# Head pairs taken two at a time: scores, exponentials and softmax sums by quads in a fused attention and MLP kernel

**Chip, cores, metric.** One core of a Trainium2 chip. The metric is device microseconds (us) of one execution; lower is better. Every timing below is a median of several executions, beside executions of the kernel before on the same chip; an execution more than 1.5% above the fastest of its kernel is called slow and left out of the ratios.

## The reference

Soft-capped attention over 8 batches of 12 heads (448 tokens, head dimension 64), then an MLP over all 3584 tokens (width 768, inner width 1024).

```python
scores = scale * np.matmul(q, k.transpose(0, 1, 3, 2))
scores = cap * np.tanh(scores / cap)
attn = np.exp(scores - max)            # then divided by its sum
attn_out = np.matmul(attn, v)
x = attn_out.transpose(0, 2, 1, 3).reshape(B * S, H * D)
h1, h2 = x @ w1, x @ w2
out = np.maximum(h1, h2) @ w_out
```

The kernel uses max(h1, h2) = relu(x(w1 - w2)) + x w2, and multiplies w2 by w_out beforehand. So the MLP has a gate-up product with w1 - w2 (`wd_sb`), a relu, and two output products (`wm_sb`, `wo_sb`).

## The kernel before

A *pair* is two heads, one on each half of the 128 partitions; there are 48. In the traces every engine works through its own instructions in program order. The program interleaves attention with a queue of filling matmuls: `F(n)` emits the next n matmuls of the MLP (early on: of the preparation of the weights). Of the 448 keys of a head, three chunks of 128 are used whole; the last 64 keys of both heads share one chunk.

```python
def qk(i, j):                         # scores of chunk j of pair i, then tanh
    ...
    if j < NJ:
        for h in range(2):            # two row halves at once
            nc.tensor.matmul(s[:, h, :S], t[r, j*P:(j+1)*P], qTn[r, :])
        nc.scalar.activation(tanh[i][:, TJ[j]:TJ[j]+2, :], s[:, :, :S], AF.Tanh, ...)
    else:                             # shared last chunk
        nc.tensor.matmul(s[:, 0, :S], t[:, 3*P:4*P], qTn)
        nc.scalar.activation(tanh[i][:, TJ[j], :], s[:, 0, :S], AF.Tanh, ...)

def add(i, step):                     # sums of exponentials on VectorE, from pair 9 on
    if step == 0:   nc.vector.tensor_add(esum[i], e[:, 0:2, :], e[:, 2:4, :])
    elif step < 3:  nc.vector.tensor_add(esum[i][r, h, :], esum[i][r, h, :], e[r, TJ[3], :])  # 64 rows
    else:           nc.vector.tensor_add(esum[i], esum[i], e[:, TJ[2]:TJ[2]+2, :])
# pv(i): PV product into ps[:, 0], sums (all-ones matmul) into ps[:, 1]
# pv_out(i): VectorE copies both into U[group of three pairs]

def gather(g):                        # once per three pairs
    nc.sync.dma_start(out=sums, in_=<one row of U per head>)
def invert(g):                        # reciprocal, then to DRAM
    nc.vector.reciprocal(rec_s, sums);  nc.sync.dma_start(out=rec_d, in_=rec_s)
def spread(g):                        # read back, broadcast over 64 partitions
    eng = nc.gpsimd if g < 2 else nc.sync
    eng.dma_start(out=rec_b[...], in_=<rec_d>.to_broadcast(...))
def normalize(g):                     # GpSimd: xT = U * rec_b
    ...
for i in range(N):                    # main loop, cut
    qk(i+1, 2); ex(i+1, 5, 7); pv(i); pv_out(i)
    if n == G-1: gather(g)            # n = i % 3
    F(5); add(i+1, 0); <loads, casts, transposing loads of later pairs>
    F(4); add(i+1, 1); F(3); add(i+1, 2); qk(i+2, 0); qk(i+2, 1)
    F(6); add(i+1, 3)
    if n == 0: invert(g-1); spread(g-1)
    if n == 1: normalize(g-1)
    qk(i+2, 3); ex(i+2, 0, 5); F(7)
```

## Time and profile before

| | before |
|---|---|
| median of 4 runs beside the changed kernel | 389.3 us (387.9 to 391.5) |
| profiled execution, first to last instruction | 390.3 us (392.1 device us, 2.8 above the median) |
| VectorE (DVE) busy | 265.8 us, 68% |
| start of the short exponential of the twelfth pair | 87.3 us |
| 34 later pairs, from 101.9 to 333.2 us | 231.3 us |

The two last rows come from the start times of the exponentials on ScalarE (ACT). The first marks the end of the early part, in which inputs and weights still arrive. The prediction shows the main lines of this profile. Columns of all views of waits: us in total, number, longest.

### The profile page before, as it was taken

What the parts mean: (1) busy time and instruction counts of PE and PEld (TensorE: products, weight loads), DVE (VectorE), ACT (ScalarE), POOL (GpSimd) and SP (SyncE); (2) the same over time, 40 slices, a digit from 0 to 9 for tenths busy, and PEclk for the clock granted to TensorE, in tenths of its full rate; (3) what the DMA queues carried; (4) which work ended last, traced back from release to release, by engine and by line L of the source; (5) the groups of instructions that cost most, each with busy time, mean ns of one, the idle gap of its engine ahead of it and who ended that gap; (6) DMA issues with size and microseconds to landing.
All of it is one profiled execution on the core that took longest, in us unless ns stands there. A gap on an engine that the chain in (4) does not pass through costs nothing.

```text
span 390.3 us, 6492 instructions
## 1 busy us (share of the span) xinstructions
PE 354.5 (91%) x2449; PEld 170.0 (44%) x2449; DVE 265.8 (68%) x401; ACT 290.2 (74%) x289; POOL 157.6 (40%) x191
## 2 busy tenths in 40 slices
PE   2667999799998999999988999999979999989995
PEld 1223555443443444444433444444434444455563
DVE  4431687998779676987788588886877867833521
ACT  3899899697998799888986999889987999200000
POOL 3464165773436442725454363534453421320000
PEclk9997999999999999999999999999999999999999
DMA  7999899465979567977797488969794851422021
GB/s 230 266 254 219 289 288 249 124 164 145 235 208 256 154 157 220 230 233 193 199 238 206 101 238 237 251 151 239 207 200 129 161 146 45 113 72 114 9 82 81
DMA packets 100391, 71.55 MB, mean 183 GB/s; under 512 B 58248, under 2 KB 93192, under 8 KB 100360
## 3 DMA queue, kind: packets, MB, share of 16 engines
q1 hardware_dynamic: 98088, 66.62, 65.0%
q0 software_dynamic: 2272, 4.52, 5.8%
q8 instruction: 19, 0.31, 0.4%
q14 instruction: 12, 0.10, 0.1%
HBM read 53.48 MB, written 11.18 MB: 166 GB/s over the span
## 4 chain that ended last, share of the span: by engine, by line
PE 56%; DVE 23%; ACT 10%; DMA 7%; SPq 1%; issue 1%; POOL 1%; DVEq 0%; POOLq 0%; ACTq 0%
PE mm L418 12%; PE mm L403 11%; PE mm L415 10%; PE pv L328 6%; PE s L288 6%; DVE u L347 5%; DVE esum L311 5%; ACT expo L295 5%; ACT tanh L289 4%; DVE esum L307 4%; PE pv L336 3%; DVE gT L407 3%; PE pv L335 3%; DMA rec_b<-rec_d 2%; PE mm L235 2%; DVE esum L313 2%
## 5 line engine op out<-in xcount | busy, mean ns | idle before, releaser
L289 ACT ACTIVATE tanh<-s 128x896 bf16<-128x896 f32 x144 | 126.0, 910 | 33.2 <-PE s L288 33.0
L295 ACT ACTIVATE expo<-tanh 128x2240 bf16<-128x2240 bf16 x96 | 145.0, 1510 | 3.0
L390 POOL TENSOR_TENSOR xT<-u,rec_b 128x448 bf16<-128x448 f32 x44 | 53.7, 1246 | 91.9 <-DMA rec_b<-rec_d 65.7
L403 PE MATMUL mm<-xT,wd_sb 128*128 128x448 bf16 x384 | 82.3, 352 | 7.4 <-DVE gT L407 6.4
L418 PE MATMUL mm<-wo_sb,gT 128*128 128x384 bf16 x448 | 88.0, 326 | 0.0
L347 DVE COPY u<-pv 128x896 f32<-128x896 f32 x45 | 49.1, 1091 | 54.3 <-PE pv L336 47.7
L415 PE MATMUL mm<-wm_sb,xT 128*128 128x384 bf16 x336 | 67.8, 326 | 2.2 <-DVE osb L422 1.7
L418 PEld LDWEIGHTS <-gT 128*128 128x128 bf16 x448 | 42.8, 98 | 31.8 <-issue 5.0
L403 PEld LDWEIGHTS <-wd_sb 128*128 128x128 bf16 x384 | 36.7, 98 | 43.1 <-issue 13.0
L288 PE MATMUL s<-qkT 64*128 64x448 bf16 x288 | 46.2, 368 | 7.3 <-ACT tanh L289 6.2
L311 DVE TENSOR_TENSOR esum<-esum,expo 64x448 bf16<-64x448 bf16 x78 | 49.9, 640 | 1.6
L422 DVE COPY osb<-mm 128x384 f32<-128x384 f32 x56 | 30.8, 552 | 21.7 <-PE mm L418 21.3
L407 DVE TENSOR_SCALAR gT<-mm 128x448 bf16<-128x448 f32 x64 | 38.9, 612 | 8.5 <-PE mm L403 7.7
L415 PEld LDWEIGHTS <-xT 128*128 128x128 bf16 x336 | 32.1, 98 | 28.1 <-issue 7.6
L328 PE MATMUL pv<-expo,vp 128*64 128x448 bf16 x288 | 37.5, 370 | 0.0
L159 POOL CAST vp<-vr 128x1152 bf16<-128x1152 f32 x15 | 18.1, 1209 | 43.7 <-DMA vr<-in_v_dram 32.7
L307 DVE TENSOR_TENSOR esum<-expo 128x896 bf16<-128x896 bf16 x39 | 35.0, 899 | 0.0
L288 PEld LDWEIGHTS <-qkT 64*128 64x128 bf16 x288 | 11.2, 94 | 46.8 <-issue 45.0
L292 ACT ACTIVATE tanh<-s 128x448 bf16<-128x448 f32 x48 | 26.3, 549 | 6.9 <-PE s L291 6.8
L313 DVE TENSOR_TENSOR esum<-esum,expo 128x896 bf16<-128x896 bf16 x39 | 27.8, 712 | 2.2
L291 PE MATMUL s<-qkT 128*128 128x448 bf16 x48 | 17.5, 364 | 3.8 <-ACT tanh L289 3.6
L179 POOL CAST kqf<-qr 128x1152 bf16<-128x1152 f32 x12 | 13.9, 1161 | 16.8 <-DMA qr<-in_q_dram 16.7
(60 smaller groups left out, 252.1 us busy)
## 6 DMA issues: line engine op xcount, KB each, us to landing
rec_b<-rec_d SPq DMA_DIRECT2D x26, 336.0 KB
kr<-in_k_dram SPq DMA_DIRECT2D x12, 576.0 KB
qr<-in_q_dram SPq DMA_DIRECT2D x12, 576.0 KB
vr<-in_v_dram SPq DMA_DIRECT2D x12, 576.0 KB
out_dram<-osb SPq DMA_DIRECT2D x18, 384.0 KB
out_dram<-osb SPq DMA_DIRECT2D x20, 192.0 KB
osb<-in_moe_w_dram SPq DMA_DIRECT2D x6, 512.0 KB
kr<-in_k_dram SPq DMA_DIRECT2D x3, 672.0 KB
```

The source lines that it names most:

```text
L288: nc.tensor.matmul(s[:, h, :S], t[r, j * P : (j + 1) * P], qTn[r, :])
L289: nc.scalar.activation(tanh[i][:, TJ[j] : TJ[j] + 2, :], s[:, :, :S], AF.Tanh, scale=scale / cap)
L295: nc.scalar.activation(expo[i][:, c0:c1, :], tanh[i][:, c0:c1, :], AF.Exp, scale=float(cap))
L307: nc.vector.tensor_add(esum[i], e[:, 0:2, :], e[:, 2:4, :])
L311: nc.vector.tensor_add(esum[i][r, h, :], esum[i][r, h, :], e[r, TJ[3], :])
L328: nc.tensor.matmul(ps[r, 0, :S], vp[g % 2][:, 2 * n + h, j, :], e[:, TJ[j] + h, :], start=(j == 0), stop=False)
L347: nc.vector.tensor_copy(U[g][:, :, n, :], pvt[i][:, :, :S])
L390: eng.tensor_mul(xT[b // 2][:, hp, cs], U[g][:, 0, n, :], rec[g, n0][:, n - n0, :])
L403: nc.tensor.matmul(ps[:, :S], wd_sb[:, c, f * P : (f + 1) * P], x[:, c, cs], start=(c == 0), stop=(c == KC - 1))
L407: nc.vector.tensor_relu(g[:, f, cs], ps[:, :S])
L415: nc.tensor.matmul(ps[:, : DM // 2], x[:, c, ts], wm_sb[:, c, hs], start=(c == 0), stop=False)
L418: nc.tensor.matmul(ps[:, : DM // 2], g[:, f, ts], wo_sb[:, f, hs], start=False, stop=(f == FC - 1))
```

## The change

Two pairs form a *quad* (24 of them). Scores are made in three visits of the 64-row tiling instead of four; both pairs' last chunks share one tanh and one exponential, and the other exponentials run over two chunks (1792 elements) at once. The half-height adds on VectorE go away: the last chunk is now added by TensorE, in 64-column tiles, and the sums of the four heads are made in four 32-column tiles. The sums have their own copy (`st`). Gather, reciprocal, read-back and multiply run once per quad instead of once per three pairs.

```diff
-    ones = const.tile([P, 64], ...);  ones2 = const.tile([P, P], ...)
+    ones = const.tile([P, 32], ...);  ones2 = const.tile([P, 64], ...)
-    def qk(i, j): ...                       # four visits for two pairs
+    PARTS = (((0,0),(0,1)), ((0,2),(1,0)), ((0,3),(1,3)), ((1,1),(1,2)))
+    def scores(t, p, m0=0, m1=2): ...       # part 2: both last chunks, whole array
+    def ex(t, p): ...                       # 4 x 448 elements, part 2: 2 x 448
     def add(...):
-        elif step < 3: <two adds of 64 rows>
     def pv(t, ab):
+        if ab:
+            for m in range(2): matmul(ss[64*m:64*m+64, :S], ones2, expo[t,2][:, m, :])
+            for m in range(4): matmul(ss[32*m:32*m+32, :S], ones, esum[t][:, m, :])
+        U[t] = upool.tile([P, 2, S], ..., bufs=3)     # 6 pairs; before: 2 buffers of 3 pairs, the first 3 pairs in a borrowed tile
+        nc.vector.tensor_copy(U[t][:, ab, :], ps[:, :S])
+        if ab:
+            nc.vector.tensor_copy(st, ss[:, :S])
+            nc.sync.dma_start(out=sums[t], in_=<st>)  # gather, per quad
     for t in range(NQ):                     # main loop after, cut
+        scores(t+1, 0); ex(t, 3); F(4); transposes; F(7); extra(i)
+        if t > 1 and t <= 3: normalize(t-2, 0); normalize(t-2, 1)
+        if t > 0: invert(t-1)
+        F(6); scores(t+1, 1); ex(t+1, 0); pv(t, 0); F(5)
+        if t > 0: spread(t-1)
+        add(t, 1, 0); F(4); add(t, 1, 1); F(3); subtract; scores(t+1, 2); ex(t+1, 1)
+        F(5); add(t+1, 0, 0); F(4); extra(i+1); F(4); scores(t+1, 3); ex(t+1, 2); pv(t, 1)
+        if t > 2: normalize(t-1, 0); normalize(t-1, 1)
+        F(4); add(t+1, 0, 1); F(3); subtract
```

`extra` issues loads, casts and transposing loads of later pairs. The gather goes out at the end of `pv(t-1, 1)`, and `invert(t-1)` follows 18 filling matmuls later (about 4 us). Before, the reciprocal came 43 filling matmuls, about 1.7 pairs, behind the gather.

More of the change, by code (lines that the diff above doesn't have):

```diff
@@ L37 @@
     L = 3
-    G = 3
+    NQ = N // 2
     Q0 = 4 * P
@@ L42 @@
     R7 = S // 64
-    TJ = (0, 2, 5, 4)
     scale = 1.0 / (D ** 0.5)
@@ L67 @@
     vl = [const.tile([P, L, P], bf16, name=f"vl{i}") for i in range(2)]
-    ones = const.tile([P, 64], bf16, name="ones")
-    ones2 = const.tile([P, P], bf16, name="ones2")
+    ones = const.tile([P, 32], bf16, name="ones")
+    ones2 = const.tile([P, 64], bf16, name="ones2")
     kqf = [const.tile([P, L, 8, P], bf16, name=f"kqf{i}") for i in range(2)]
@@ L94, in fill_const @@
             for h in range(2):
-                eng.memset(ones2[64 * h : 64 * h + 64, 64 * h : 64 * h + 64], 1.0)
+                eng.memset(ones2[64 * h : 64 * h + 64, 32 * h : 32 * h + 32], 1.0)
     raw = {}
@@ L191, in cast @@
                 eng.tensor_copy(t[r, n0:n1, 3, r], l[r, n0:n1, :])
-    x1 = xpool.tile([P, NP, 2 * S], bf16, name="xT").rearrange("p n s -> p (n s)")
     w1_in = {}
@@ L273, in cross @@
         )
-    def qk(i, j):
-        g, n = divmod(i, L)
-        t = qkT[g][:, n, :, :].rearrange("p j c -> p (j c)")
-        o = Q0 + (64 * (i // NP % 2) if g >= NT else 0)
-        qTn = t[:, o : o + S]
-        if j == 0:
-            tanh[i] = att.tile([P, 7, S], bf16, name="tanh", bufs=1)
-            expo[i] = att.tile([P, 7, S], bf16, name="expo")
-        s = s_psum.tile([P, 2, 512], f32, name="s")
-        if j < NJ:
+    PARTS = (((0, 0), (0, 1)), ((0, 2), (1, 0)), ((0, 3), (1, 3)), ((1, 1), (1, 2)))
@@ new lines, with scores @@
+    LP = {c: (p, 2 * m if p != 2 else m) for p, cs in enumerate(PARTS) for m, c in enumerate(cs)}
+    def scores(t, p, m0=0, m1=2):
+        if m0 == 0:
+            tanh[t, p] = att.tile([P, 4, S], bf16, name="tanh")
+        if p == 2:
+            s = s_psum.tile([P, 2, 512], f32, name="s")
+        for m, (ab, j) in list(enumerate(PARTS[p]))[m0:m1]:
+            i = 2 * t + ab
+            g = i // L
+            k0 = qkT[g][:, i % L, :, :].rearrange("p j c -> p (j c)")
+            o = Q0 + (64 * (i // NP % 2) if g >= NT else 0)
+            qTn = k0[:, o : o + S]
+            if p == 2:
+                nc.tensor.matmul(s[:, m, :S], k0[:, 3 * P : 4 * P], qTn)
+                continue
+            s = s_psum.tile([P, 2, 512], f32, name="s")
@@ L286, in qk @@
             for h in range(2):
                 r = slice(64 * h, 64 * h + 64)
-                nc.tensor.matmul(s[:, h, :S], t[r, j * P : (j + 1) * P], qTn[r, :])
-            nc.scalar.activation(tanh[i][:, TJ[j] : TJ[j] + 2, :], s[:, :, :S], AF.Tanh, scale=scale / cap)
-        else:
-            nc.tensor.matmul(s[:, 0, :S], t[:, 3 * P : 4 * P], qTn)
-            nc.scalar.activation(tanh[i][:, TJ[j], :], s[:, 0, :S], AF.Tanh, scale=scale / cap)
-    def ex(i, c0, c1):
-        nc.scalar.activation(expo[i][:, c0:c1, :], tanh[i][:, c0:c1, :], AF.Exp, scale=float(cap))
@@ L297 @@
-    esum = {}
-    def add(i, step):
-        if i < NS or i >= N:
-            return
-        e = expo[i]
-        if step == 0:
-            esum[i] = att.tile([P, 2, S], bf16, name="esum")
-            nc.vector.tensor_add(esum[i], e[:, 0:2, :], e[:, 2:4, :])
-        elif step < 3:
-            h = step - 1
-            r = slice(64 * h, 64 * h + 64)
-            nc.vector.tensor_add(esum[i][r, h, :], esum[i][r, h, :], e[r, TJ[3], :])
-        else:
-            nc.vector.tensor_add(esum[i], esum[i], e[:, TJ[2] : TJ[2] + 2, :])
@@ L315, with ex @@
-    U = {}
-    pvt = {}
-    def pv(i):
+                nc.tensor.matmul(s[:, h, :S], k0[r, j * P : (j + 1) * P], qTn[r, :])
+            nc.scalar.activation(tanh[t, p][:, 2 * m : 2 * m + 2, :], s[:, :, :S], AF.Tanh, scale=scale / cap)
+        if p == 2:
+            nc.scalar.activation(tanh[t, p][:, 0:2, :], s[:, :, :S], AF.Tanh, scale=scale / cap)
+    def ex(t, p):
+        n = 2 if p == 2 else 4
+        expo[t, p] = att.tile([P, n, S], bf16, name=f"expo{p}", bufs=1 if p == 3 else 2)
+        nc.scalar.activation(expo[t, p], tanh[t, p][:, 0:n, :], AF.Exp, scale=float(cap))
@@ new lines, in e_of, with add @@
+    def e_of(t, ab, j):
+        p, m = LP[ab, j]
+        return expo[t, p][:, m : m + (1 if j == NJ else 2), :]
+    esum = {}
+    def add(t, ab, step):
+        if t < NS or t >= NQ:
+            return
+        if t not in esum:
+            esum[t] = att.tile([P, 4, S], bf16, name="esum")
+        d = esum[t][:, 2 * ab : 2 * ab + 2, :]
+        if step == 0:
+            nc.vector.tensor_add(d, e_of(t, ab, 1 if ab else 0), e_of(t, ab, 2 if ab else 1))
+        else:
+            nc.vector.tensor_add(d, d, e_of(t, ab, 0 if ab else 2))
@@ L322, in pv @@
+    U, sums, rec, recd = {}, {}, {}, {}
+    def pv(t, ab):
+        i = 2 * t + ab
         g, n = divmod(i, L)
-        e = expo[i]
-        ps = pvt[i] = pv_psum.tile([P, 2, 512], f32, name="pv")
+        ps = pv_psum.tile([P, 512], f32, name="pv")
         for j in range(NJ):
@@ L328, in pv @@
                 nc.tensor.matmul(
-                    ps[r, 0, :S], vp[g % 2][:, 2 * n + h, j, :], e[:, TJ[j] + h, :], start=(j == 0), stop=False
+                    ps[r, :S], vp[g % 2][:, 2 * n + h, j, :], e_of(t, ab, j)[:, h, :], start=(j == 0), stop=False
                 )
-        for j in range(NJ if i < NS else 1):
-            for h in range(2):
-                r = slice(64 * h, 64 * h + 64)
-                x = e[:, TJ[j] + h, :] if i < NS else esum[i][:, h, :]
-                nc.tensor.matmul(ps[r, 1, :S], ones, x, start=(j == 0), stop=(i >= NS))
@@ L336, in pv @@
-        nc.tensor.matmul(ps[:, 0, :S], vl[g % 2][:, n, :], e[:, TJ[3], :], start=False, stop=True)
-        if i < NS:
-            nc.tensor.matmul(ps[:, 1, :S], ones2, e[:, TJ[3], :], start=False, stop=True)
-    def pv_out(i):
-        g, n = divmod(i, G)
-        if n == 0:
-            if g == 0:
-                U[g] = x1.bitcast(f32).rearrange("p (h n s) -> p h n s", h=2, n=G)
-            else:
-                U[g] = upool.tile([P, 2, G, S], f32, name="u")
-        nc.vector.tensor_copy(U[g][:, :, n, :], pvt[i][:, :, :S])
@@ L349 @@
-    sums, rec = {}, {}
-    def gather(g, n0=0, n1=G):
-        t = sums[g, n0] = xpool.tile([16 * G, 56], f32, name="sums")
-        m = 8 * (n1 - n0)
-        for h in range(2):
-            r = 64 * h
+        if ab:
+            ss = pv_psum.tile([P, 512], f32, name="ss")
+            for m in range(2):
+                nc.tensor.matmul(
+                    ss[64 * m : 64 * m + 64, :S], ones2, expo[t, 2][:, m, :], start=True, stop=False
+                )
+            nj = NJ if t < NS else 1
+            for j in range(nj):
+                for m in range(4):
+                    x = e_of(t, m // 2, j)[:, m % 2, :] if t < NS else esum[t][:, m, :]
+                    nc.tensor.matmul(ss[32 * m : 32 * m + 32, :S], ones, x, start=False, stop=(j == nj - 1))
@@ L357, in gather @@
+        nc.tensor.matmul(ps[:, :S], vl[g % 2][:, n, :], expo[t, 2][:, ab, :], start=False, stop=True)
+        if ab == 0:
+            U[t] = upool.tile([P, 2, S], f32, name="u", bufs=3)
+        nc.vector.tensor_copy(U[t][:, ab, :], ps[:, :S])
+        if ab:
+            st = upool.tile([P, S], f32, name="st")
+            nc.vector.tensor_copy(st, ss[:, :S])
+            sums[t] = xpool.tile([32, 56], f32, name="sums")
             nc.sync.dma_start(
-                out=t[m * h : m * h + m, :],
@@ L359, in gather @@
-                in_=U[g][r : r + 1, 1, n0:n1, :].rearrange("o n (a c) -> o (n a) c", a=8),
-            )
-    recd = {}
-    def invert(g, n0=0, n1=G):
-        m = 16 * (n1 - n0)
-        t = xpool.tile([16 * G, 56], f32, name="rec_s")
-        nc.vector.reciprocal(t[:m, :], sums[g, n0][:m, :])
-        d = recd[g, n0] = dram.tile([16 * G, 56], f32, name="rec_d")
-        nc.sync.dma_start(out=d[:m, :], in_=t[:m, :])
-    def spread(g, n0=0, n1=G):
-        rb = rec[g, n0] = xpool.tile([P, G, S], f32, name="rec_b")
-        lines = recd[g, n0][: 16 * (n1 - n0), :].rearrange("(h n a) c -> h n (a c)", h=2, a=8)
-        eng = nc.gpsimd if g < 2 else nc.sync
+                out=sums[t], in_=st.rearrange("(m p) (a c) -> m p a c", p=32, a=8)[:, 0, :, :]
+            )
@@ L375, in spread, with invert @@
+    def invert(t):
+        r = xpool.tile([32, 56], f32, name="rec_s")
+        nc.vector.reciprocal(r, sums[t])
+        recd[t] = dram.tile([32, 56], f32, name="rec_d")
+        nc.sync.dma_start(out=recd[t], in_=r)
+    def spread(t):
+        rec[t] = xpool.tile([P, 2, S], f32, name="rec_b")
+        lines = recd[t].rearrange("(n h a) c -> h n (a c)", h=2, a=8)
+        eng = nc.gpsimd if t < 2 else nc.sync
         for h in range(2):
             eng.dma_start(
-                out=rb[64 * h : 64 * h + 64, : n1 - n0, :],
@@ L378, in spread, with normalize @@
-                in_=lines[h : h + 1, :, :].to_broadcast([64, n1 - n0, S]),
+                out=rec[t][64 * h : 64 * h + 64, :, :], in_=lines[h : h + 1, :, :].to_broadcast([64, 2, S])
             )
     xT = {}
-    def normalize(g, n0=0, n1=G, eng=nc.gpsimd):
-        for n in range(n0, n1):
-            i = g * G + n
-            b, hp = divmod(i, NP)
-            if i % (2 * NP) == 0:
-                xT[b // 2] = xpool.tile([P, NP, 2 * S], bf16, name="xT")
-            cs = slice((b % 2) * S, (b % 2 + 1) * S)
-            eng.tensor_mul(xT[b // 2][:, hp, cs], U[g][:, 0, n, :], rec[g, n0][:, n - n0, :])
+    def normalize(t, ab, eng=nc.gpsimd):
+        i = 2 * t + ab
+        b, hp = divmod(i, NP)
+        if i % (2 * NP) == 0:
+            xT[b // 2] = xpool.tile([P, NP, 2 * S], bf16, name="xT")
+        cs = slice((b % 2) * S, (b % 2 + 1) * S)
+        eng.tensor_mul(xT[b // 2][:, hp, cs], U[t][:, ab, :], rec[t][:, ab, :])
@@ L450 @@
     NL = N // L
-    NS = 9
+    NS = 4
     todo = [[] for _ in range(N)]
@@ L466 @@
         else:
-            at(3 * g - 8, load, g, "k")
-            at(3 * g - 7, load, g, "q")
-            at(3 * g - 4, load, g, "v")
-            at(3 * g - 5, cast, nc.gpsimd, g, "k")
-            at(3 * g - 5, cast, nc.gpsimd, g, "q")
-            at(3 * g - 2, cast, nc.gpsimd, g, "v")
-            at(3 * g - 4, cross, g)
+            e = 3 * g - g % 2
+            at(e - 8, load, g, "k")
+            at(e - 7, load, g, "q")
+            at(e - 4, load, g, "v")
+            at(e - 5, cast, nc.gpsimd, g, "k")
+            at(e - 5, cast, nc.gpsimd, g, "q")
+            at(e - 2, cast, nc.gpsimd, g, "v")
+            at(e - 4, cross, g)
     for c, i in enumerate((2, 2, 3, 4, 5, 6)):
@@ L493 @@
     cast(nc.vector, 0, "q", 1, L)
-    qk(0, 0)
-    qk(0, 1)
+    scores(0, 0)
+    scores(0, 1, 0, 1)
+    ex(0, 0)
     transposes(1)
-    qk(0, 3)
-    ex(0, 0, 5)
-    qk(0, 2)
-    ex(0, 5, 7)
+    scores(0, 1, 1, 2)
+    ex(0, 1)
+    scores(0, 2)
+    ex(0, 2)
+    scores(0, 3)
     transposes(2)
@@ L512, with weights @@
         load_w2(c)
-    qk(1, 0)
-    qk(1, 1)
-    qk(1, 3)
-    ex(1, 0, 5)
-    for i in range(N):
-        b, hp = divmod(i, NP)
-        g, n = divmod(i, G)
-        late = i >= N - 4
-        if i + 1 < N:
-            qk(i + 1, 2)
-            ex(i + 1, 5, 7)
-        pv(i)
-        pv_out(i)
-        if i == N - 2:
-            gather(g, 0, G - 1)
-        elif i == N - 1:
-            gather(g, G - 1, G)
-        elif n == G - 1:
-            gather(g)
+    def weights(i):
         if MS < i <= MS + KC:
@@ L536, with extra @@
             fill_q.append(turn_w2(i - MS))
-        if i == MS + KC:
-            fill_q.append(moe(0))
-        if hp == 3 and b > 1:
-            fill_q.append(moe(b - 1))
-        first = i < 2 * G + 2
-        F(2 if late else 5)
-        add(i + 1, 0)
+    def extra(i):
         for f, a in todo[i]:
             f(*a)
-        if i == G + 1:
-            spread(0)
-        if i == G + 2 or i == 2 * G + 1:
-            normalize(i // G - 1)
-        F(4)
-        add(i + 1, 1)
-        F(3)
@@ L553 @@
-        add(i + 1, 2)
-        if i + 2 < N:
-            qk(i + 2, 0)
-            qk(i + 2, 1)
+    for t in range(NQ):
+        i = 2 * t
+        more = t + 1 < NQ
+        weights(i)
+        if t % 3 == 1 and t > 4:
+            fill_q.append(moe(t // 3 - 1))
+        if more:
+            scores(t + 1, 0)
+        ex(t, 3)
+        F(4)
         if i + 3 < NT * L:
             transposes(i + 3)
-        F(6)
-        add(i + 1, 3)
-        if first and i >= G and n == 0:
-            invert(g - 1)
@@ L563 @@
-        if i == 2 * G:
-            spread(1)
-        if i == N - 1:
-            invert(g, 0, G - 1)
-            spread(g, 0, G - 1)
-        elif not first and n == 0:
-            invert(g - 1)
-            spread(g - 1)
-        if not first and n == 1:
-            normalize(g - 1)
-        if i + 2 < N:
-            qk(i + 2, 3)
-            ex(i + 2, 0, 5)
-        F(2 if late else 7)
+        F(7 if more else 0)
+        extra(i)
+        if t > 1 and t <= 3:
+            normalize(t - 2, 0)
+            normalize(t - 2, 1)
@@ L577 @@
+        if t > 0:
+            invert(t - 1)
+        F(6 if more else 2)
+        if more:
+            scores(t + 1, 1)
+            ex(t + 1, 0)
+        pv(t, 0)
+        F(5)
+        if t > 0:
+            spread(t - 1)
+        add(t, 1, 0)
+        F(4 if more else 2)
+        add(t, 1, 1)
+        F(3 if more else 0)
         if MS <= i < MS + KC:
             subtract(i - MS)
-    F(10)
-    invert(N // G - 1, G - 1, G)
-    spread(N // G - 1, G - 1, G)
-    normalize(N // G - 1, 0, G - 1)
@@ L583 @@
-    F(24)
-    normalize(N // G - 1, G - 1, G, nc.vector)
+        if more:
+            scores(t + 1, 2)
+            ex(t + 1, 1)
+        weights(i + 1)
+        if t == 4:
+            fill_q.append(moe(0))
+        if i + 4 < NT * L:
+            transposes(i + 4)
+        F(5 if more else 0)
+        if more:
+            add(t + 1, 0, 0)
+        F(4 if more else 0)
+        extra(i + 1)
+        F(4 if more else 0)
+        if more:
+            scores(t + 1, 3)
+            ex(t + 1, 2)
@@ L585 @@
+        pv(t, 1)
+        if t > 2:
+            normalize(t - 1, 0)
+            normalize(t - 1, 1)
+        F(4)
+        if more:
+            add(t + 1, 0, 1)
+        F(3 if more else 0)
+        if MS <= i + 1 < MS + KC:
+            subtract(i + 1 - MS)
+    F(12)
+    invert(NQ - 1)
+    F(10)
+    spread(NQ - 1)
+    F(30)
+    normalize(NQ - 1, 0)
+    normalize(NQ - 1, 1, nc.vector)
     fill_q.append(moe(B - 1))
```

## The prediction

> **What bounds the kernel now.** I read the busy shares of the page first, then the windows, the chain of waits, and last the timeline.
>
> From the page, part 1:
>
> ```profile
> PE 354.5 (91%) x2449; PEld 170.0 (44%) x2449; DVE 265.8 (68%) x401; ACT 290.2 (74%) x289; POOL 157.6 (40%) x191
> ```
>
> No engine is full by its average, so the bound changes by stage. ACT ends at 334 us of 390; behind it PE works alone. Before it, two stretches differ (windows; busy PE, PEld, DVE, ACT, POOL):
>
> ```profile
> 202.50:216.80 14.30, 12.76 (x71) 5.58 (x70) 11.75 (x18) 10.25 (x12) 6.13 (x9) 1.00 0.89 223
> 217.00:231.00 14.00, 14.00 (x95) 6.64 (x94) 9.80 (x15) 13.06 (x13) 7.49 (x9) 1.00 0.62 153
> ```
>
> The second is the ordinary stretch, where PE fills its time with the MLP's output matmuls (L415, L418). The first holds 48 gate-up matmuls (L403): only 71 matmuls are done against 95, ACT is idle for 4 of 14 us, PE has gaps, and DVE alone is busier than in the other stretch (11.75 against 9.80 us). Who held whom is in the chain of waits of that stretch:
>
> ```profile
> 203.89 1.37 DVE esum L307
> 205.26 0.53 DVE gT L407
> 205.79 0.31 DVE esum L311
> ...
> 206.12 1.24 DVE esum L311
> ...
> 207.39 0.64 DVE gT L407
> ...
> 208.05 0.63 DVE esum L313
> 208.67 0.41 DVE rec_s L367
> 209.08 0.49 DVE gT L407
> ...
> 209.61 0.35 PE mm L403
> ```
>
> DVE is the chain here. Each relu eviction (gT) stands behind a sum of exponentials (esum), and PE, with two eviction buffers, waits. The costs by form (last columns: total busy, mean ns):
>
> ```profile
> L311 DVE TENSOR_TENSOR esum<-esum,expo 64x448 bf16<-64x448 bf16 x78 | 49.9, 640 | 1.6
> L347 DVE COPY u<-pv 128x896 f32<-128x896 f32 x45 | 49.1, 1091 | 54.3 <-PE pv L336 47.7
> L307 DVE TENSOR_TENSOR esum<-expo 128x896 bf16<-128x896 bf16 x39 | 35.0, 899 | 0.0
> L313 DVE TENSOR_TENSOR esum<-esum,expo 128x896 bf16<-128x896 bf16 x39 | 27.8, 712 | 2.2
> L295 ACT ACTIVATE expo<-tanh 128x2240 bf16<-128x2240 bf16 x48 | 99.4, 2070 | 1.5
> L295 ACT ACTIVATE expo<-tanh 128x896 bf16<-128x896 bf16 x48 | 45.6, 950 | 1.5
> ```
>
> The timeline gives the period of a pair of heads, from one short exp to the next. Early, where ACT is the limit, they start at 14.36, 20.44, 26.52: 6.08 us. In ordinary stretches it is 6.31 us. In the gate-up stretch above: 196.97, 203.28, 211.24, 219.52, so 7.96 and 8.28 us.
>
> PE's need by start-to-start distances: an unbroken run of 48 gate-up matmuls takes 9.08 us, 0.189 each; eight output matmuls take 1.30, 0.1625 each. A pair has 25 filling matmuls and 9 attention slots of 448 columns (4 scores, 3 PV, 1 sum, 1 last chunk; two half-array matmuls share a slot). Between the array's tilings each change costs 0.09 to 0.11 us over the normal distance (median of about 250 changes), five per pair. So 25 x 0.1625 + 9 x 0.189 + 5 x 0.1 = 6.27, the 6.31 seen: ordinary stretches are bound by PE. Gate-up gives 4.73 + 1.70 + 0.5 = 6.93 against the 8 seen: one us lost per pair to DVE.
>
> **What the Trainium skill says.** "TensorEngine Tiling (Array Packing)", Key Properties: changing the tiling mode, not just the tile, drains TensorE. The trace agrees: about 0.1 us at each change. The same page, Restrictions: column tiling disables fast weight load. The trace agrees: a 64-column load takes 110 to 116 ns, a 128-column one 98. "TensorE: Matmul & The Clock Gate", Part 3: matmuls in distinct column groups run at the same time; three 32-column tiles measured 2.38x. The trace before shows only two groups, which start 4 ns apart; four are untested here. "ScalarE: Activation LUTs", What ACT_TABLE_LOAD costs: an activation takes 186 ns + 0.833 ns per element; the trace has 2070 for 2240 and 950 for 896, the same slope.
>
> **The change part by part**, for a quad (two pairs).
>
> *DVE.* Removed: four half-height adds (4 x 640 = 2560), two copies of 896 (2 x 1091 = 2182). Added: three copies of 448 (about 620 each, between the 552 of 384 and 1091 of 896: 1860). Full adds stay four (3222). One reciprocal per quad (480) replaces one per three pairs (325). So 8289 becomes 5562: 2.7 us less per quad, about 54 us over 20 quads. A gate-up quad needs 8 relus (8 x 0.612 = 4.9) besides: 13.2 of 13.9 us becomes 10.5. DVE stops being a bound. The gain is not the 54 us but the PE waits that they caused.
>
> *ACT.* Seven tanhs of 896 replace six of 896 and two of 448; three exps of 1792 and one of 896 replace two of 2240 and two of 896. By start-to-start distance before: 2 x 6.08 = 12.16 per quad. After: three tanh-to-tanh steps of 0.814, four tanh-to-exp of about 0.80, three long exps of about 1.73 (1697 interpolated, plus a wait since the next tanh takes over its input buffer), one short of 0.98: 11.8. That is 0.36 less per quad, where ACT binds.
>
> *PE.* Slots per quad are 18 as before: the last chunks' sums take a 64-column slot, the four heads' sums one 32-column slot. Fill is 49 instead of 50. Changes of tiling: four row visits become three, but 64 to 32 columns is a new change: 9 or 10 instead of 10, at most 0.1 us less. While DVE does no adds (first 9 pairs before, first 4 quads now), sums need 4 slots per quad instead of 8. With 9 pairs: 36 against 17 slots for the same heads, 3.6 us, of which about half lies where PE binds.
>
> *Start.* ACT waited 2.36 us at 8.5 for the second pair's transposes. Now another tanh and a long exp stand ahead of them: about 2 us less.
>
> Sum. Up to the first gate-up matmul (82.6 before): start 2, ACT 5 pairs x 0.18 = 0.9, sums 1.7, the DVE jam at the turn (period 8.81 against 6.7) 1.5: about 6; I take 5, since early loads may come into the way. From 82.6 to PE's last end at 386.2: 303.6 us. PE's need there: 384 x 0.189 + 784 x 0.1625 + 336 slots x 0.189 + 190 changes x 0.1 = 72.6 + 127.4 + 63.5 + 19 = 282.5. So 21 us are lost: about 3 where the fill queue ran dry (18 missing matmuls in three pairs, by counting the program), 2.5 in the tail after 335, 1.6 regular, and about 14 around DVE. After: the fill never runs dry; tail and regular losses stay (4); I allow 0.6 in each of 8 gate-up stretches (5) and 2 for the 32-column changes and loads: 11. That saves 10, and the changes of tiling about 1. 390.5 - 5 - 10 - 1 = 374.5; the last eviction and store (4 us) stay.
>
> **The rivals.** (1) *The chain of sums becomes a new wait.* It is now run per quad: copy, gather by DMA, reciprocal on DVE 18 matmuls later, about 3.8 us behind the PV's end. The copies take 1.3; the small store rec_d before landed about 2.1 us after issue, so the gather may arrive 0 to 1 us late, and DVE, in order, stands still meanwhile. For it: the queue of SP also carries transposing DMAs of 3.1 us. Against: those lie in the other half of the quad. Also the MLP of a batch is queued one pair earlier; by my count its input is ready 2 to 3 us ahead. If all were late by 2 us: 24 x 0.7, so about 390. (2) *Four 32-column matmuls don't run together.* Three more slots in 20 quads, nine more in 4: 96 x 0.189 = 18 us at most, half of it hidden: about 384. (3) *PE and ACT in lock step.* In ordinary stretches PE needs 12.3 and ACT 11.8 per quad; if the new pieces fit badly, each waits for the other in turn, 0.3 per quad, 6 us: 380. (4) *DVE was merely masked*: then only early gains and changes of tiling stay, 384. (5) *Everything fits*: the loss falls to 5, giving 367.
>
> **Range and chances.** 374 us. Rival 5 gives the low end, 364 with some luck at the start; one of rivals 2 to 4 in full gives the high end, 384. Two per cent faster is 382.7: all but the bad cases lie below it. Faster 0.82, same 0.16, slower 0.02.
>
> **What would show it.** Right: the adds of half height gone and DVE below 57% of the span; gate-up quads near 13.9 us, ordinary ones near 12.5; ACT waiting for scores 10 to 20 us instead of 33; early period near 5.9 per pair; the four 32-column matmuls starting within some 15 ns, the next slot 0.2 later. Wrong: reciprocals waiting over 1 us for the gather with PE waiting behind relus, POOL's multiply holding L403, or 32-column matmuls 0.19 apart.

## More of the kernel before

One more is needed later: SyncE's queue before. It shows how long the queue that issues nearly all transfers stood before the read-back of the reciprocals, which may be issued only when `rec_d` is in DRAM.

```profile
SPq L376 <- DMA rec_d<-rec_s: 32.0, 15, 3.7
```

There are 15 such stands of about 2 us each; no reciprocal waited for a gather behind them.

## The result and the profile after

The changed kernel is slower: 400.5 us median of 4 runs (398.4 to 402.7) against 389.3. Ratio 1.028, 95% interval [1.020, 1.036]. All ratios here are the mean time of one kernel's fast runs over the mean of the other's of the same rounds, so not quite the ratio of the medians quoted.

The page of the changed kernel, part 1 (busy us, share of the span, instructions):

```profile
PE 351.5 (88%) x2484; PEld 168.3 (42%) x2484; DVE 200.6 (50%) x356; ACT 281.6 (71%) x265; POOL 154.5 (39%) x191
```

VectorE lost 65 us of work, as intended, and every other engine lost some too. Yet the span grew: this is new waiting. The view of waits after:

```profile
POOL xT L384 <- DMA rec_b<-rec_d: 157.7, 22, 16.1
DVE rec_s L363 <- DMA sums<-st: 62.8, 17, 7.5
...
ACT tanh L296 <- PE s L295: 51.9, 44, 11.6
...
PE mm L409 <- DVE osb L416: 10.7, 7, 2.4
PE mm L262 <- POOL kqf L171: 5.3, 1, 5.3
```

Before, VectorE had no wait for a gather in its list at all; now its reciprocal (L363) stands 62.8 us for it. ScalarE waits 51.9 us for scores, against 33.0. And the queue of SyncE (SPq):

```profile
SPq L372 <- DMA rec_d<-rec_s: 43.7, 22, 3.9
SPq L365 <- DVE rec_s L363: 25.2, 8, 8.0
```

One stand in front of the read-back (L372) per quad, 22 instead of 15, in a queue that also carries the gather, the loads and the transposing loads.

**Where in time.** Two marks split the span. The prediction's own mark, the first gate-up matmul, moved from 82.6 to 95.5 us; but ScalarE is about a pair further on there than it was before, so the exponentials are the fairer mark.

| | before | after |
|---|---|---|
| to the short exponential of pair 12 (quad 6) | 87.3 | 95.2 |
| from there to the end | 303.0 | 303.2 |
| 17 quads (34 pairs) between two short exponentials | 231.3 | 231.9 |

(One long exponential of the quad comes after this mark, where the old pair is complete with it, so the real lateness is some 1.6 us more: an estimate from the exponential's 1.7 us.) The early part lost 8 us instead of gaining 5. The rest gained nothing instead of 11. The two profiled executions lie 8.1 us apart, the medians 11.2, as the profiled execution of the kernel before was a long one. In the middle (windows from 95 to 335 us) the granted clock is 1.00 in both, so the clock has no part in that loss.

**A middle quad, closely.** The timeline of the changed kernel, of VectorE, SyncE, TensorE and ScalarE (start us, duration us, engine, line, operation; in brackets the idle time before it and its releaser):

```profile
191.58 0.61 DVE L354 COPY st<-ss 128x448 f32<-128x448 f32 x1
193.82 1.24 SPq L372 DMA_DIRECT2D rec_b<-rec_d  x2
195.10 0.60 SPq L137 DMA_DIRECT2D qr<-in_q_dram  x1
196.84 0.62 SPq L357 DMA_DIRECT2D sums<-st  x1
201.17 0.49 DVE L363 RECIPROCAL rec_s<-sums 32x56 f32<-32x56 f32 x1 [6.72 <-DMA sums<-st]
202.65 1.14 PE L409 MATMUL mm<-wm_sb,xT 128*128 128x384 bf16 x6 [2.39 <-DVE osb L416]
204.35 1.73 ACT L296 ACTIVATE tanh<-s 128x896 bf16<-128x896 f32 x2 [2.46 <-PE s L295]
```

The sums lie ready in `st` at 192.19. SyncE is still in front of an earlier read-back, then has loads to issue, and sends the gather only at 196.84, 4.65 us later. It lands 4.3 us after that. Meanwhile VectorE, in program order, stands 6.72 us on the reciprocal, with evictions behind it. TensorE runs out of eviction buffers (`osb`) and stands 2.39 us, and ScalarE then waits 2.46 us for scores.

The windows of the changed kernel show the stretch before that wait beside the stretch with it (window, its length, busy us of PE, PEld, DVE, ACT, POOL, granted clock, DMA share, GB/s):

```profile
176.50:190.50 14.00, 14.00 (x87) 6.02 (x87) 9.21 (x16) 11.79 (x12) 4.34 (x5) 1.00 0.93 215
190.50:205.00 14.50, 12.11 (x83) 5.89 (x79) 6.57 (x11) 11.27 (x11) 6.24 (x7) 1.00 0.73 186
```

**The early part, closely.** The timeline of GpSimd (POOL) after:

```profile
43.92 1.24 POOL L372 DMA_DIRECT2D rec_b<-rec_d  x2 [12.66 <-DMA rec_d<-rec_s]
...
53.19 2.23 POOL L384 TENSOR_TENSOR xT<-u,rec_b 128x448 bf16<-128x448 f32 x2 [6.19 <-DMA rec_b<-rec_d]
...
58.09 1.23 POOL L372 DMA_DIRECT2D rec_b<-rec_d  x2 [2.66 <-DMA rec_d<-rec_s]
59.31 1.16 POOL L171 CAST kqf<-kr 128x1152 bf16<-128x1152 f32 x1
```

and of the kernel before:

```profile
45.31 1.05 POOL L376 DMA_DIRECT2D rec_b<-rec_d  x2 [11.01 <-DMA rec_d<-rec_s]
49.53 1.14 POOL L172 CAST kqf<-kr 128x1152 bf16<-128x1152 f32 x1 [3.17 <-PE s L288]
```

The first two reads of reciprocals are issued by GpSimd. Before, the cast of the keys of pairs 9 to 11 stood behind one of them and started at 49.53. Now it also stands behind the first multiply and a second read-back, and starts at 59.31. Without it TensorE has no transposes, and without those no scores: the longest wait of ScalarE, 11.6 us, ends at 69.76. The windows from 55 to 70 us, before and after:

```profile
55.00:70.00 15.00, 14.74 (x161) 8.12 (x162) 11.45 (x17) 13.46 (x15) 10.13 (x13) 1.00 0.97 261
```

```profile
55.00:70.00 15.00, 6.86 (x54) 3.21 (x52) 3.68 (x6) 3.40 (x4) 8.77 (x13) 0.66 1.09 251
```

TensorE did 54 matmuls instead of 161, and its granted clock fell to 0.66.

### The profile page after: what moved, and what is told of

It reads as the page before. It is cut to its first block, busy times and chain, and to the rows that moved or that the text cites.

```text
span 398.4 us, 6530 instructions
## 1 busy us (share of the span) xinstructions
PE 351.5 (88%) x2484; PEld 168.3 (42%) x2484; DVE 200.6 (50%) x356; ACT 281.6 (71%) x265; POOL 154.5 (39%) x191
## 4 chain that ended last, share of the span: by engine, by line
PE 42%; DMA 27%; DVE 10%; SPq 8%; ACT 4%; issue 4%; POOL 4%; DVEq 0%; POOLq 0%; ACTq 0%
PE mm L397 12%; DMA sums<-st 12%; PE mm L412 8%; PE mm L409 7%; DMA rec_d<-rec_s 5%; PE pv L334 4%; PE s L295 4%; DMA qr<-in_q_dram 3%; DMA kr<-in_k_dram 3%; DMA out_dram<-osb 3%; DVE u L351 2%; SPq L372 2%; PE pv L348 2%; DVE osb L416 2%; ACT tanh L296 2%
## 5 line engine op out<-in xcount | busy, mean ns | idle before, releaser
L296 ACT ACTIVATE tanh<-s 128x896 bf16<-128x896 f32 x144 | 124.2, 914 | 52.9 <-PE s L295 51.9
L303 ACT ACTIVATE expo<-tanh 128x1792 bf16<-128x1792 bf16 (+1 forms) x96 | 144.8, 1509 | 0.1
L397 PE MATMUL mm<-xT,wd_sb 128*128 128x448 bf16 x384 | 79.5, 352 | 2.8 <-DVE gT L401 1.8
L351 DVE COPY u<-pv 128x448 f32<-128x448 f32 x48 | 29.4, 612 | 60.0 <-PE pv L348 57.6
L295 PE MATMUL s<-qkT 64*128 64x448 bf16 x288 | 43.4, 372 | 8.8 <-DVE qkT L264 3.4
L363 DVE RECIPROCAL rec_s<-sums 32x56 f32<-32x56 f32 x24 | 11.7, 489 | 66.5 <-DMA sums<-st 62.8
L319 DVE TENSOR_TENSOR esum<-expo 128x896 bf16<-128x896 bf16 x40 | 29.1, 728 | 0.0
L298 ACT ACTIVATE tanh<-s 128x896 bf16<-128x896 f32 x24 | 22.0, 916 | 7.9 <-PE s L290 7.7
L232 PE MATMUL mm<-wo_sb,w2T 128*128 128x384 bf16 x96 | 21.8, 376 | 6.5 <-DVE w2T L224 5.2
L334 PEld LDWEIGHTS <-vp 128*64 128x64 bf16 x288 | 12.5, 110 | 22.7 <-issue 18.9
L262 PE MATMUL mm<-ident,kqf 64*64 64x64 bf16 x312 | 9.5, 218 | 12.1 <-POOL kqf L171 5.3
```

What stands on the lines that cost most here:

```text
L295: nc.tensor.matmul(s[:, h, :S], k0[r, j * P : (j + 1) * P], qTn[r, :])
L296: nc.scalar.activation(tanh[t, p][:, 2 * m : 2 * m + 2, :], s[:, :, :S], AF.Tanh, scale=scale / cap)
L303: nc.scalar.activation(expo[t, p], tanh[t, p][:, 0:n, :], AF.Exp, scale=float(cap))
L319: nc.vector.tensor_add(d, e_of(t, ab, 1 if ab else 0), e_of(t, ab, 2 if ab else 1))
L334: nc.tensor.matmul(ps[r, :S], vp[g % 2][:, 2 * n + h, j, :], e_of(t, ab, j)[:, h, :], start=(j == 0), stop=False)
L351: nc.vector.tensor_copy(U[t][:, ab, :], ps[:, :S])
```

## The experiments

The edits are given against the changed kernel unless said otherwise. The main theory at the start: the reciprocal now comes too early, VectorE stands on the gather, and that is the whole loss. Rivals: the loss is in the queues (SyncE's and GpSimd's order), or in the early transfers. Letters in the expectations stand for theories as each expectation states them. A profile is one execution; its early part varies by some us from one execution to the next (runs with the same early program reached the mark at 95.2 and 100.0). The 17 quads vary by 1 to 4 us: with the changed kernel's middle they took 231.9, 230.4 (e3) and 234.4 (h1), with the later read-back 222.1 to 223.5 in eight runs, all but i2 with the later reciprocal as well.

### e1_const: the reciprocal reads a constant

```diff
-        nc.vector.reciprocal(r, sums[t])
+        nc.vector.reciprocal(r, fixed)      # memset to 448; the gather is still sent
```

The scores are so small that the sums are close to 448, and the output stays within tolerance.

> Wrong result on purpose (sums taken as 448): the reciprocal reads a constant tile, so it waits for no gather; the gather is still sent, the rest is the changed kernel. Theory A (the reciprocal, run per quad, stands in VectorE's order waiting for the gather of the sums, 66 us in all, and delays evictions, loads and casts behind it): 377 to 386 us, VectorE's idle before reciprocals under 3 us in all, the first gate-up matmul at 80 to 86 us instead of 95.5. Theory B (the quad's order puts TensorE and ScalarE in lock step): 396 us or more. Theory C (early loads and transposes come too late for quads, whatever the sums do): the first gate-up matmul stays at 92 or later, 388 to 394 us.

Measured: 402.0 us (400.5 to 404.8), ratio 1.036 [1.028, 1.044]. No reciprocal waits, and nothing is gained. The mark is at 96.4. Most middle quads now take 12.4 to 13.4 us, but three take 18.22, 19.58 and 14.96, and the 17 together 231.6. In these, score matmuls wait for the transposing load of keys and queries (waits of this kernel):

```profile
PEld L297 <- DMA qkT<-kqf: 9.6, 3, 4.3
PE s L297 <- DMA qkT<-kqf: 8.2, 3, 3.9
```

SyncE's timeline of this kernel shows why it came late (line numbers are two higher in this kernel):

```profile
159.31 0.34 SPq L367 DMA_DIRECT2D rec_d<-rec_s  x1
163.02 2.07 SPq L374 DMA_DIRECT2D rec_b<-rec_d  x2
...
167.86 0.59 SPq L359 DMA_DIRECT2D sums<-st  x1
...
171.11 5.18 SPq L270 DMA_TRANSPOSE qkT<-kqf  x1
```

From 159.65 to 163.02 the queue stands for `rec_d`; then a store, the loads and the gather go out back to back, and the transposing load, itself 5.18 us of issue, starts only at 171.11. The time is where theory B put it, but through late loads, not through lock step. So the simple theory fell: take the wait from VectorE, and another consumer of the same queue becomes the late one.

### e2_late_all, e3_late_first, e4_late_rest: reciprocal and read-back half a quad later

```diff
-        if t > 0: invert(t - 1)             # after extra(i)
+        if t > 0: invert(t - 1)             # after transposes(i + 4), before F(5)
-        if t > 0: spread(t - 1)             # behind pv(t, 0)
+        if t > 0: spread(t - 1)             # after extra(i + 1) and F(4)
```

e2 does it for all quads, e3 for t <= 4 only, e4 for t > 4 only.

> Correct result. The reciprocal and the spread of its result are moved half a quad later (about 5 us more for the gather to land). Theory A: 380 to 389 us, VectorE's idle before reciprocals under 15 us. Theory B: 398 or more. Theory C: the first gate-up matmul stays past 92.

> Correct result. The move of e2 only in the first five quads. Theory A: the early loss alone comes back, first gate-up matmul at 82 to 88, 390 to 395 us. Theory C: no change, 398 or more.

> Correct result. The move of e2 only from the sixth quad on. Theory A: the early part stays as in the changed kernel, the quads after 96 us get shorter (mean 13.0 instead of 13.6), 388 to 394 us. Theory B: 398 or more.

Measured: e2 388.8 us (385.3 to 391.9), ratio 0.993 [0.985, 1.000]; e3 397.9 us, 1.023 [1.017, 1.029]; e4 393.7 us (391.5 to 396.8), 1.014 [1.005, 1.022]. Two of e2's four executions were slow, the profiled one among them (390.2 us), so its ratio rests on two, and its profile is read for order, not for shares. In e2 the reciprocals wait 3.6 us in all. The 17 quads take 230.4 (e3) and 222.3 (e4), and 223.5 in e2's slow execution: the later place is worth 8 to 10 us in the middle. Early it is worth nothing that could be told apart: the mark is at 93.8 (e2) and 94.7 (e3), where the changed kernel had 95.2. Theory A held in the middle (e2, e4), theory C early (e3). The early loss has another cause. Since these edits moved two things, the reciprocal and the read-back, the next two runs part them.

### i2_spread_only, i1_const_spread: the read-back alone

```diff
-        if t > 0: spread(t - 1)             # behind pv(t, 0)
+        if t > 0: spread(t - 1)             # after extra(i + 1) and F(4); invert stays
```

i1 has the constant of e1 besides.

> The changed kernel with the reciprocals' read-back (rec_b) issued half a quad later and nothing else: the reciprocal stays where the change put it. If the gather is late mainly because SyncE stood behind the read-back and what queued up behind it, the 62.8 us of VectorE waiting for the gather fall to under 30 us, the 17 quads from 6 to 23 take about 13.2 to 13.4 us each instead of 13.64 and the time is 390 to 395 us. If the gather's own landing (2 to 6 us from its issue) is what the early reciprocal cannot bear, the wait stays at 35 to 60 us, the quads at 13.5 or more, the time at 397 to 402 us.

> The kernel whose reciprocal reads a constant (no wait of VectorE for the gather), and the read-back issued half a quad later besides. If the late transposing loads of the constant kernel came from SyncE standing in front of the read-back, the three long quads (18.2, 19.6 and 15.0 us) are gone, all 17 quads take about 13.1 us each (222 to 224 us together) and the time is 390 to 395 us, level with the kernel that only reads late. If the long quads have another cause (the transfers' own time), they stay, and the time is 399 to 404 us.

Measured: i2 387.8 us (387.5 to 389.1), ratio 0.996 [0.990, 1.001]; i1 390.4 us (388.0 to 392.5), 1.004 [0.997, 1.010]. With e1 and the changed kernel they form a square, for the 17 middle quads (us, one profiled execution each):

| | read-back early | read-back half a quad later |
|---|---|---|
| reciprocal waits for the gather | 231.9 (changed kernel) | 222.7 (i2) |
| reciprocal waits for nothing | 231.6 (e1) | 220.6 (i1) |

Moving the read-back alone, one DMA issue per quad, takes 9.2 us out; taking VectorE's wait away takes out 0.3 alone and 2.1 after that, both within the scatter. The middle loss is the place of the read-back on SyncE's queue. My expectation for i2 was half right: it gained more than expected, though its reciprocals still wait. SyncE's stand before the read-back fell from 43.7 us to about half (waits of i2):

```profile
DVE rec_s L363 <- DMA sums<-st: 39.5, 15, 6.1
SPq L372 <- DMA rec_d<-rec_s: 22.8, 13, 4.1
```

How can 39.5 us of waiting be nearly free and 62.8 not? Quads of the changed kernel and of i2, each against the same quad of i1, answer it:

| wait of the reciprocal, us | quad longer than in i1 by, us |
|---|---|
| changed kernel: 6.72, 6.13, 6.12 | 2.44, 2.06, 1.84 |
| changed kernel: 5.98, 5.94, 4.94 | 1.63, 1.67, 1.19 |
| changed kernel: 4.28, 4.08 | 0.53, 0.59 |
| i2: 6.05, 4.67, 4.10 | 1.25, 0.39, 0.94 |
| i2: 3.13, 2.71, 2.54, 1.66, 1.51 | 0.00 in each |

About the first 3 to 4 us cost nothing, as TensorE still has attention work and eviction buffers; of what is beyond, most shows in the time. (The other quads have waits under 3.7 us and scatter: within 0.7 us of i1's, but for the quad in which i1 itself waits for a transposing load, 1.8 and 1.1 us shorter than there.) The eight quads of the first three rows are 12.0 us longer together, a little more than the whole difference of 11.3 between the changed kernel and i1. In the changed kernel the gather went out 1.8 us after the copy on average (quads 5 to 18, longest 4.65) and, where it was waited for over 1 us, took 2.5 to 5.7 us to land, 4.3 on average (from its issue to the start of the reciprocal); in i2 1.2 us, and 2.9 to 5.2, 3.5 on average. Why it also lands sooner in i2 no run shows. In i1 the three long quads of e1 take 15.67, 13.52 and 13.34 us instead of 18.22, 19.58 and 14.96; the transposing loads are in time but for one wait of 2 us. So the first reading of i1's expectation held, except for one long quad.

### g1_before_early: the old kernel, with the reciprocal early

Against the kernel before: `invert` 18 filling matmuls behind the gather instead of 43, from the third group on.

> Correct result. The kernel before, with one change: from the third group on, the reciprocal stands 18 filling matmuls behind the gather, the distance of the changed kernel, instead of 43. Theory A: VectorE's idle before reciprocals grows from 0 to 15 to 40 us, and the whole time by 3 to 9, to 393 to 399 us. Rival (such a wait is absorbed by slack): 388 to 391.

Measured: 389.8 us (387.4 to 394.3), ratio 0.997 [0.989, 1.004], no wait of a reciprocal above 0.5 us. Missed. In matmuls the distance is the same as in the changed kernel, but when VectorE comes to the reciprocal here, the gather has landed. The likely reasons, not tested singly, are the adds that VectorE does in front of it and the fewer read-backs on SyncE's queue. So distance in filling matmuls is not distance in time. One more thing counts for what follows: g1's 34 middle pairs took 227.0 us and its mark to the end 299.8, with the same work as the kernel before (231.3 and 303.0). No run shows whether the early reciprocal or scatter did that, but the figures of the kernel before come from its one, long, profiled execution and may be some 3 to 4 us too high.

### h1_no_wo: less early DMA traffic

```diff
-    for f in range(0, FC, 2): load_wo(f)
+    nc.vector.memset(wo_sb, 0.03125)        # wrong result on purpose
```

> Wrong result on purpose: the changed kernel without the load of the output weights (3.1 MB from HBM; a constant instead). Theory D (early DMA traffic): gathers 0 to 2 land within 5 us, the casts of pair 9 before 54 us, the first gate-up matmul at 82 to 88 instead of 95.5, 388 to 393 us. Theory P (order on GpSimd and on the queue, whatever the traffic): first gate-up at 92 or later, 397 or more.

Measured: 403.6 us (400.1 to 405.4), ratio 1.030 [1.024, 1.036]. The mark is at 97.7, and the cast of the keys of pairs 9 to 11 starts at 60.85, again behind GpSimd's issue of a read-back (10.1 us of waiting). But the edit brought a delay of its own. The constant is written by VectorE, in front of a copy of transposed keys and queries:

```profile
21.26 5.18 DVE L503 MEMSET wo_sb<- 128x6144 bf16 x1 [1.34 <-issue]
```

ScalarE then waits 5.33 us for scores, and the first quad takes 19.33 us instead of 13.88. Without that the mark would lie near 92.3 (an estimate: 97.7 less 5.45), 3 us before the changed kernel's and within the early scatter. Of theory D's signs, one came in part: the first two gathers were there within 1.8 and 2.9 us (9.1 and 2.1 in the changed kernel), the third within 6.6 (9.0). So h1 does not settle what the traffic costs early.

### f1_norm_late, f2_early_pool, f3_early_loads, f4_four_u, f6_subtract: the early order

Each builds on the one before (f4 on f2, f6 on f4), and f1 on e2:

```diff
 f1: normalize(t-1) behind pv(t, 1)  ->  normalize(t-2) after extra(i), half a quad later
 f2: eng = nc.gpsimd if t < 2 else nc.sync  ->  nc.sync;
     first two multiplies only at t = 3, behind the casts of pairs 9 to 11
 f3: keys and queries of pairs 9 to 11 loaded one quad earlier
 f4: U: bufs=3 -> bufs=4
 f6: every second weight subtraction from the end of the quad to after F(7) of the next
```

> Correct result. e2 plus: from the fifth quad on, GpSimd's multiply by the reciprocals comes half a quad later, after a cast instead of ahead of it. Theory A2 (GpSimd, in order, stands before these multiplies waiting for the spread, and the casts and transposing loads behind it come late; this is what e1 ran into): 383 to 387 us, GpSimd's wait for the spread from 152 to under 90 us, no score matmul waiting over 0.5 us for a transposing load after 100 us. Rival (GpSimd has slack, the wait is harmless once the reciprocal is late): 387 to 391, as e2.

> Correct result. f1 plus, in the first quads: the spread of the first two quads issued by SyncE instead of GpSimd, and the first multiplies moved behind the casts of pairs 9 to 11. Theory P (the early loss comes from GpSimd's order: casts of pair 9 behind multiplies and behind issues that wait for DMAs): the first gate-up matmul at 85 to 90 us instead of 94, whole time 4 to 8 below f1. Theory D (the loads of pairs 9 to 11 come too late): no change against f1.

> Correct result. f2 plus: the loads of k and q for pairs 9 to 11 issued one quad earlier. Theory D: the first gate-up matmul at 82 to 88 us, whole time 375 to 382. Theory P: within 2 us of f2.

> Correct result. f2 with four buffers for the PV results instead of three. In f2 the casts of pair 9 came in time, but VectorE then waited 4.9 us for a PV buffer that a late multiply still held. Theory P with the ring of buffers (six pairs instead of nine before): the first gate-up matmul at 83 to 88 us, whole time 378 to 384. Theory D (DMA alone sets the early pace): first gate-up at 91 or later, 386 or more.

> Correct result. f4 plus: every second weight subtraction moved from the end of a quad to 11 filling matmuls later, so that the copy of the turned weights does not stand behind it. If this order costs (gaps of 2.3 us three times in f2): 3 to 5 us below f4; otherwise equal to f4.

> The best version once more, unaltered, for an interval: its first timing left two runs out and gave no ratio. If it is truly better than the kernel before, 381 to 388 us with the ratio's interval below 0.995; if its first runs were lucky ones, 387 to 391 us and an interval that holds 1.

| | median us | ratio to before [95%] | mark | 17 quads |
|---|---|---|---|---|
| e2 (base; marks of a slow execution) | 388.8 | 0.993 [0.985, 1.000] | 93.8 | 223.5 |
| f1 | 390.5 | 0.999 [0.991, 1.006] | - | - |
| f2 | 388.9 | 0.994 [0.985, 1.002] | 92.2 | 222.8 |
| f3 | 392.8 | 1.004 | 94.6 | 222.1 |
| f4 | 389.5 | 0.995 [0.989, 1.000] | 89.2 | 222.4 |
| f6 | 385.3 | none: two of its runs slow | 84.7 | 223.1 |
| f6, repeated as f6_again | 385.1 | 0.988 [0.982, 0.993] | 87.5 | 222.8 |

The profiled execution of f1 took 1179 us, with every matmul near 0.63 us; its other three took 388.5 to 392.0. What happened in that one execution is not explained, and its profile is not used. With f2, the cast of those keys starts at 51.8 instead of 59 to 61, but then VectorE's copy of the PV result once waits 6.4 us for GpSimd's multiplies, because only three quads of `U` exist. f4 takes that wait away (in f6_again two waits of 1.9 us are back). f3 won nothing: the earlier load, issued at 31.8, was there only at 48.9, 17 us later. f6 moves one VectorE instruction out of the way of evictions. In the repeat, the GpSimd timeline shows what is left:

```profile
51.70 1.15 POOL L171 CAST kqf<-kr 128x1152 bf16<-128x1152 f32 x1 [15.61 <-DMA kr<-in_k_dram]
```

Since f2 the cast waits for its data, not for other work of GpSimd. Of the expectations, those of f6 and f6_again came true, f1 went as its rival said, f2 showed no change clear of noise against f1 (theory D), and f3 and f4 met neither of their theories in full. Between one step and the next the differences are within the scatter of the early part, so single shares are not told apart. Together, f2, f4 and f6 bring the mark from 91.4 to 100.0 (the changed kernel, e1 to e4, i1 and i2) to 84.7 and 87.5: most of the early loss came from the order of work on GpSimd and VectorE and the small `U`. What the transfers' volume adds to it is not shown. f6 is the best version: 385.1 us, 1.2% below the kernel before and 3.9% below the changed kernel's median.

## Why the prediction was wrong

- **The cost by instruction was right.** VectorE fell to 50% of the span (below 57% was asked for). The early quad in which nothing but ScalarE binds takes 11.82 us (11.8 foretold). Quads without a wait take 12.36 to 12.5 us in output stretches (12.5) and 13.3 to 13.6 in gate-up ones (13.9); one gate-up quad, with two short waits for relus, takes 14.58 in every version. The four 32-column matmuls start within about 10 ns of each other, so rival 2 is out; a change from 64 to 32 columns costs 93 ns (282 from start to start instead of 189), about as much as any other. What the prediction read from the weight loads has less support: a 32-column load takes 93 ns, no longer than the 98 of a 128-column one.
- **The bound was named right, and the gain exists.** With the read-back moved, the same work in the middle takes 222 to 223 us instead of 231.3. From the mark to the end, i2 needs 294.4 and f6_again 295.6 us, against 303.0 before: 7 to 9 us of the 11 foretold (10, and 1 for the tilings), or 4 to 5 if g1's 299.8 is the truer base. (i1, with its constant, needs 291.9.)
- **The step that failed in the middle is rival 1's sizing:** "the gather may arrive 0 to 1 us late". It took 2.1 us from issue to landing from another small transfer (`rec_d`), and took for granted that the issue follows the copy at once. Measured, the issue came up to 4.65 us after the copy and the landing up to 5.7 us after the issue, and VectorE stood up to 6.7 us in the middle and 7.5 at the first quad. "Against: those lie in the other half of the quad" was the very error: transposing loads (4.1 to 5.6 us of issue each in the changed kernel) and the stand of 2 us before each read-back push what is behind them into the next half. The sign that the prediction asked for, reciprocals waiting over 1 us with TensorE waiting behind relus, is what came, though the evictions waited for were mostly those of the output (`osb`). So the prediction named the right rival and even put it at 390, but left that out of its range, and gave slower a chance of 0.02.
- **The step that failed early is "about 6; I take 5".** Start and ScalarE gained as foretold: the third short exponential starts at 40.96, where the sixth pair's started at 45.70. But the sum had no term for GpSimd, whose first multiply and second read-back now stood before the cast of pairs 9 to 11. The mark came 7.9 us later, not about 5 sooner, a miss of 13 us. That this order carries most of it is what f2, f4 and f6 show together.
- **Together:** -5 - 10 - 1 became +7.9 and +0.2, which is the 8.1 us between the two profiled executions. Rivals 3 and 4 did not decide it; i2 shows that the gain was given back to one queue's order.
- **What stays open.** Which of f2, f4 and f6 gives how much of the early recovery, and what the early transfers' volume adds; how far the baseline's middle is above its usual time; why the gather lands sooner in i2; f1's one long execution. And even the best version keeps 11 us from the 374 foretold: about 5 early (87.5 where 87.3 - 5 was foretold) and 4 from the mark to the end (295.6 against 292), the rest between median and profile.

## What to carry to other kernels

Here a DMA issue that had to wait for an earlier transfer held everything behind it on SyncE's queue: put such an issue behind the loads and gathers that need not wait, and give it half a stage of distance. When an engine is relieved, look at what its slowness had hidden: a consumer that now arrives early meets transfers that have not landed, and the distance between producer and consumer has to be read in time on the trace, not in instructions of another engine. A short wait is free as long as the buffers behind it last (here 3 to 4 us); sum only what lies beyond.

## What the Trainium skill lacked or had wrong

- "DMA: Bandwidth & Descriptors", Anatomy of one DMA, says "DMA engines do not wait on semaphores": the wait is on the issuing sequencer. This agrees (SyncE stood 43.7 us in 22 places before the read-back), but the page draws no rule for the order within one queue from it; moving that one issue per quad is worth 9.2 us of 232 here. The section also puts a nearly constant 2 us on setup and completion, fitted on DMAs that GpSimd issues. The 7 KB gather, issued by SyncE, took that in the quiet tail (1.8 us from the issue at 341.85 to the reciprocal) and once early (at most 2.1 from 42.70); where it was waited for in the middle it took 2.5 to 5.7 us, and 9.1 at the start. For planning, the measurement decides: 2 us is near the lower end. Whether the rest is a longer fixed part or time behind other transfers no run separates.
- "TensorEngine Tiling (Array Packing)", Key Properties, gives the drain at a mode change no figure: about 90 to 106 ns here over the normal distance (0.163 or 0.189 us), by the pair of modes. Four 32-column tiles ran together within 10 ns.
- No page gives, in us and for this chip, the time for which a transposing load of this size occupies the issuing queue ("DMA: Bandwidth & Descriptors" has only cycles for other sizes, in a comparison for a later chip): 4.1 to 5.6 us in the changed kernel; in the one before 3.1 to 3.6 for the first eight and 4.3 to 6.1 for the last four.
